# Six added matrix products between a kernel's last product and TensorE's jump to the program's end

## The chip, the cores and the metric

The kernel runs on one core of a Trainium2 chip (trn2). The metric is the device time of one execution in microseconds; lower is better. A core has five engines that run their own instruction streams side by side: TensorE (matrix products, PE in the rows, with its weight loads as PEld), VectorE (DVE), ScalarE (ACT), GpSimd (POOL) and SyncE (SP, which here only starts transfers). Each engine has a sequencer that hands the instructions of its stream to the engine; rows of the sequencer carry a q behind the engine's name (PEldq, POOLq). The engines wait for each other through counting semaphores, and move data between memory and chip through 16 DMA engines that several queues share.

## What is computed

The reference is a block-sparse attention over 4 batches of 768 positions with 8 heads of 64, followed by a mixture of 8 experts in which each token goes to one expert:

```python
def reference(**kwargs):
    attn_out = _attn_ref(**attn_kwargs)          # window of 16 and 24 block summaries, softmax, times v
    x = attn_out.transpose(0, 2, 1, 3).reshape(B, S, H * D)
    return _moe_ref(x=x, **moe_kwargs)
...
# _moe_ref, per token: e is the best expert, or the one before if a local gate says so
h = np.maximum(x[b, s] @ w1[e], 0.0)             # 512 -> 1024
out[b, s] = p[e] * (h @ w2[e])                   # 1024 -> 512
```

## The kernel before

The first half of the program is the attention; the second half sorts the 3072 tokens by expert into blocks of 128 rows and runs the expert layers block by block. A block's rows are gathered (`gather`), turned (`tx`), multiplied with the expert's first weights (`pair_1`, `quad`, `single_parts.mm1`), passed through a relu (`relu`, or an activation in `mm1`), multiplied with the second weights (`second`, `single_parts.mm2`), scaled by the gate and scattered to their rows of the output (`store`, `scatter`). Every weight and every input of a product is held as a high and a low part, so that one product of the mathematics is three on TensorE: `mm`, lines 1147 (high times high), 1148 (high times low) and 1149 (low times high), each 128 x 128 by 128 x 512.

The order of the work is written out by hand: each engine executes its instructions as the code issues them, and a layer under the code adds the semaphore waits. How many blocks there are depends on the data. `run` holds two versions of the second half: the usual one (line 1616, `tc.If(...) as usual`), which is the one executed here, and a general one behind `usual.Else()` in line 1625. The general one follows the usual one in each engine's stream, so every engine leaves the usual version with a jump over the general one (the jump carries line 1616) to the code after both, which is the program's end.

The usual version ends in `pair_and_single`, line 1346: a pair of blocks, and with it a single last block. The last thing it does on TensorE is `mm2(range(2, 8))`, eighteen products into the bank `ya` (the `ba` of the rows). GpSimd meanwhile makes the last low parts of the second weights in four steps (line 1109), and line 1148 waits for them. The last block is not stored inside the version: `store(..., late=True)` only copies its indices and gates (lines 1155 and 1156), and behind the two versions stand, for both,

```python
nc.gpsimd.drain()                     # line 1628
self.last_rows()                      # line 1629: ya * gate -> yl on VectorE (line 1167),
                                      # then the scatter of yl on GpSimd (line 1171)
```

What stands behind the two versions has to wait for either of them. The layer under the code therefore brings each engine's count to one value at the end of both versions, and line 1167 waits until TensorE's count (PE_49) has that value, that is, until the last product of the version that ran. Then comes the program's end (line 1715), where SyncE waits for the transfers and all engines meet. Products of other lines that the text names: `few_3` (line 1224) multiplies a few rows with weights, inside a condition (line 1560).

Of the kernel before, what the change touches and what calls it, by code (L numbers as in the profile page):

```python
# [19 lines left out]
P = 128  # L20
# [68 lines left out]
class Kernel:  # L89
# [1268 lines left out]
    def run(self):  # L1358
        nc, tc = self.nc, self.tc
# [44 lines left out]
        def freed():  # L1404
            st["free"] += 1
            ask_rows()
# [32 lines left out]
        def reg(i, engines, hi):  # L1439
            return nc.values_load(self.words[0:1, i:i + 1], engines=engines, min_val=0, max_val=hi)  # L1440

        def refill(w, nxt):

            with tc.If(nxt > 0):  # L1444
                e = nc.s_assert_within(nxt - 1, 0, E - 1, skip_runtime_bounds_check_because="the branch is taken for 1 to E alone")
                for h in range(2):
                    self.fetch(st["stage"][w][:, 2048 * h:2048 * h + 2048], w, 2048 * h, 2048 * h + 2048, e)

        def split(w, chunks):
            for q in chunks:  # L1450
                eng = nc.vector if SPLIT_BY[w][q] == "V" else nc.gpsimd
                self.split(w, q * CH, q * CH + CH, st["stage"][w][:, q * CH:q * CH + CH], eng)

        def calls(n, mids={}, sure=False):

            r = {}

            def start(s):
                while "words" not in st:
                    self.small(1, True)  # L1460
                if s not in r:
                    r[s] = reg(s, (ENG.SP, ENG.Activation, ENG.DVE, ENG.Pool), 1), reg(COLS + s, (ENG.SP,), E)
                return r[s]

            def weights(w, s, chunks):
                if not EARLY <= s < SLOTS:
                    return
                new, nxt = start(s)
                with tc.If(new > 0):  # L1469
                    split(w, chunks)  # L1470
                    if chunks[-1] == NCH - 1:
                        refill(w, nxt)

            def turn(u):
                while st["next"] <= u:
                    self.small(1, True)
                if u % 2 and u >= 2 * PAIRS and not sure:
                    with tc.If(reg(u, (ENG.PE, ENG.Activation, ENG.DVE), 1) > 0):
                        self.tx(u)
                else:  # L1480
                    self.tx(u)
                freed()
                if sure and u + 1 in EMPTY:
                    assert st["next"] > u + 1
                    freed()

            mids = {j: lambda u=u: turn(u) for j, u in mids.items() if u < SLOTS}
            return mids, lambda *chunks: weights(0, n, chunks), lambda *chunks: weights(1, n, chunks)
# [17 lines left out]
        with ExitStack() as ctx:  # L1506
# [67 lines left out]
            def run(gen, n0=0):  # L1574
                n = n0
                for n, _ in enumerate(gen, n0):
                    steps.get(n, int)()
                return n + 1
# [37 lines left out]
            with tc.If(known[2 * COLS + 1] < LATE + 5 - EARLY) as usual:  # L1616
                n = 0
                for (i, k), (j, m) in zip(USUAL, USUAL[1:]):
                    if k > 2:
                        n = run(self.quad(i, k, *calls(j, dict(zip(PMU, range(j, j + m + (j == LATE)))), True)), n)  # L1620
                    elif k == 2:
                        nc.gpsimd.drain()  # L1622
                        run(self.pair_and_single(i, *calls(j)), n)
            st.update(kept)
            with usual.Else():
                slots(EARLY, LATE)
# [93 lines left out]
```

## Time and profile before

| what | us |
|---|---|
| median of 3 timed runs | 414.23 (413.96 to 414.83) |
| profiled execution, its own time | 417.37 |
| its span, first to last instruction | 415.6 |
| TensorE busy | 401.2 (97% of the span) |
| VectorE, ScalarE, GpSimd busy | 232.8, 186.9, 199.1 |
| mean granted TensorE clock | 0.997 of full speed |

The three timed runs lie 0.87 us apart. The span of the profiled execution is 1.77 us shorter than its own time, and that time is 3.14 us above the median of the timed runs. Times inside the profile count from the span's start. A busy TensorE row of 0.39 us is one product with its fill and drain; the next one starts before it has ended, so the pace is read from the starts.

### The profile page before, as it was taken

The numbers are of one execution on the slowest core, as the hardware profiler recorded it, in microseconds if no ns is written. First come the engines' busy times: TensorE is split into PE (matmuls) and PEld (weight loads), VectorE is DVE, ScalarE is ACT, GpSimd is POOL, SyncE is SP. The second block draws the span as 40 slices with busy tenths as digits, with TensorE's granted clock in tenths as the row PEclk, the third lists the DMA queues.
The fourth block names the chain that finished last, engine by engine and source line by source line (L and its number), as shares of the span: only waits on it lengthen the run. The fifth ranks groups of instructions, "written<-read, shape, count | busy, mean of one in ns | idle before, by whom it ended". The sixth has DMA issues, their size and how long they took to land. (4 is left out here: it accounts for less than half of the span.)

```text
span 415.6 us, 10447 instructions
## 1 busy us (share of the span) xinstructions
PE 401.2 (97%) x3802; PEld 332.5 (80%) x3802; DVE 232.8 (56%) x516; ACT 186.9 (45%) x461; POOL 199.1 (48%) x334
## 2 busy tenths in 40 slices
PE   7999999999999999999999999999999999999993
PEld 6678777778798888888877877888998888889882
DVE  4778978989687777685232222263537433312631
ACT  4978877788874322156221002251535422101550
POOL 7599877877769300258503310063716460010552
PEclk9999999999999999999999999999999999999998
DMA  8999999999490200857777464128353670010011
GB/s 298 412 410 407 410 401 409 386 377 334 109 353 32 84 26 0 337 224 252 267 275 250 135 222 147 83 53 294 93 186 108 233 223 35 26 53 25 2 49 34
DMA packets 21936, 83.70 MB, mean 201 GB/s; under 512 B 2638, under 2 KB 3152, under 8 KB 18800
## 3 DMA queue, kind: packets, MB, share of 16 engines
q1 hardware_dynamic: 17600, 68.49, 44.2%
q0 software_dynamic: 4128, 14.22, 9.9%
q8 instruction: 32, 0.52, 0.5%
q10 hardware_dynamic: 144, 0.20, 0.2%
q14 instruction: 32, 0.26, 0.2%
HBM read 69.43 MB, written 13.60 MB: 200 GB/s over the span
## 5 line engine op out<-in xcount | busy, mean ns | idle before, releaser
L1253 ACT ACTIVATE hT<-bs 128x256 fp32r<-128x256 f32 (+1 forms) x88 | 34.6, 394 | 116.2 <-PE bs L1292 64.2
L1255 DVE SCALAR_TENSOR_TENSOR hT<-bs,hT 128x256 fp32r<-128x256 f32 (+1 forms) x88 | 38.3, 435 | 72.1 <-ACT hT L1253 72.0
L1147 PE MATMUL ba<-h,hT 128*128 128x512 f32 x192 | 77.9, 406 | 0.0
L1149 PE MATMUL ba<-h,hT 128*128 128x512 f32 x192 | 75.1, 391 | 0.0
L1148 PE MATMUL ba<-l,hT 128*128 128x512 f32 x192 | 74.9, 390 | 0.0
L1171 POOL DMA_INDIRECT out_dram<-yo,sidx x23 | 25.7, 1116 | 77.3 <-DVE yo L1163 36.7
L1290 PE MATMUL bs<-xT,h 128*128 128x512 f32 (+1 forms) x160 | 61.1, 382 | 0.0
L1291 PE MATMUL bs<-xT,h 128*128 128x512 f32 (+1 forms) x160 | 60.6, 379 | 0.0
L1292 PE MATMUL bs<-xT,l 128*128 128x512 f32 (+1 forms) x160 | 60.6, 379 | 0.0
L1118 POOL DMA_INDIRECT xg<-x_dram,gidx x26 | 30.0, 1154 | 62.6 <-PE ba L1149 27.5
L384 ACT ACTIVATE pr<-bs,nm 128x120 f32<-128x120 f32 x192 | 52.1, 382 | 4.8 <-DVE nm L376 4.5
L1109 POOL TENSOR_TENSOR l<-stg,h 128x256 fp32r<-128x256 f32 x48 | 37.6, 814 | 14.9 <-ACT h L1101 14.8
L1149 PEld LDWEIGHTS ba<-h,hT 128*128 128x128 f32 x192 | 36.0, 188 | 7.9
L1147 PEld LDWEIGHTS ba<-h,hT 128*128 128x128 f32 x192 | 36.1, 188 | 7.2 <-issue 0.8
L307 POOL COPY vw<-gs 24x432 f32<-24x432 f32 (+2 forms) x83 | 34.2, 431 | 15.5 <-issue 10.9
L1148 PEld LDWEIGHTS ba<-l,hT 128*128 128x128 f32 x192 | 36.2, 188 | 6.4
L1101 ACT CAST h<-stg 128x1024 fp32r<-128x1024 f32 x32 | 32.5, 1048 | 12.8 <-PE ba L1149 9.9
L1104 DVE TENSOR_TENSOR l<-stg,h 128x1024 fp32r<-128x1024 f32 x20 | 30.3, 1525 | 10.9 <-ACT h L1101 10.6
L1290 PEld LDWEIGHTS bs<-xT,h 128*128 128x128 f32 x160 | 30.0, 188 | 5.4 <-PE bs L1205 0.4
L1291 PEld LDWEIGHTS bs<-xT,h 128*128 128x128 f32 x160 | 30.0, 188 | 5.1 <-DVE xT L1124 0.2
L1292 PEld LDWEIGHTS bs<-xT,l 128*128 128x128 f32 x160 | 30.0, 188 | 5.0
L405 PE MATMUL ba<-vw,pt 121*64 121x76 f32 x768 | 32.5, 233 | 1.2 <-DMA vt<-in_vT 0.7
(271 smaller groups left out, 676.9 us busy)
## 6 DMA issues: line engine op xcount, KB each, us to landing
stg<-in_w SPq DMA_DIRECT2D x16, 1024.0 KB, 5.7
vw<-in_vW SPq DMA_DIRECT2D x16, 768.0 KB, 10.5
raw<-in_w SPq DMA_DIRECT2D x8, 1024.0 KB, 8.2
x_dram<-xs SPq DMA_DIRECT2D x8, 876.0 KB, 9.6
kp<-in_kT SPq DMA_DIRECT2D x16, 384.0 KB, 7.8
q<-in_qT SPq DMA_DIRECT2D x16, 384.0 KB
vt<-in_vT SPq DMA_DIRECT2D x16, 384.0 KB, 9.2
wst<-in_w SPq DMA_DIRECT2D x8, 512.0 KB, 9.2
```

The source lines that it names most:

```text
L307: nc.gpsimd.tensor_copy(out=bass.AP(dst.tensor, dst.offset, [dst.ap[0], (step, planes), (4, NW), (1, m)]), in_=bass.AP(src.tensor, src.off ...
L384: nc.scalar.activation(out=pr[:, h, u, :], in_=sp[:, h, u, :], func=AF.Exp, bias=nm[:, h, u:u + 1], scale=1.0)
L405: nc.tensor.matmul(out=ap[64 * c:64 * c + 64, u, h], lhsT=pt[0:W + 1, h, u, 64 * c:64 * c + 64], rhs=vw[n % NVW][0:W + 1, PL * h:PL * h + ...
L1109: eng.tensor_tensor(out=lo[:, p], in0=src[:, p], in1=hi[:, p].bitcast(F32), op=ALU.subtract)
L1147: nc.tensor.matmul(out=ps, lhsT=ah, rhs=wh, start=first, stop=False)
L1148: nc.tensor.matmul(out=ps, lhsT=ah, rhs=wl, start=False, stop=False)
L1149: nc.tensor.matmul(out=ps, lhsT=al, rhs=wh, start=False, stop=last)
L1253: self.nc.scalar.activation(out=h, in_=ps, func=AF.Relu)
L1255: self.nc.vector.scalar_tensor_tensor(out=l, in0=ps, scalar=0.0, in1=h.bitcast(F32), op0=ALU.max, op1=ALU.subtract)
L1290: nc.tensor.matmul(out=ps, lhsT=wh, rhs=xh[k], start=(k == 0), stop=False)
L1291: nc.tensor.matmul(out=ps, lhsT=wh, rhs=xl[k], start=False, stop=False)
L1292: nc.tensor.matmul(out=ps, lhsT=wl, rhs=xh[k], start=False, stop=(k == KT - 1))
```

## The change

Inside the usual version, behind the loop over the blocks, TensorE gets six products more. They read a part of `hT[1]` and of the first weights, both in place for long, and write the same bank of the pool "t" six times; nothing reads that bank afterwards. Their form is that of line 1147 (128 x 128 by 128 x 512, high parts). Nothing else is changed. The lines behind it move down by three, so that the program's end is line 1718 instead of 1715.

```diff
@@ -1621,6 +1621,9 @@
                     elif k == 2:
                         nc.gpsimd.drain()
                         run(self.pair_and_single(i, *calls(j)), n)
+                idle = self.bank("t")
+                for _ in range(6):
+                    nc.tensor.matmul(out=idle, lhsT=self.hT[1][:, 0, 0, 0:P], rhs=self.hi[0][:, 0:512], start=True, stop=True)
             st.update(kept)
             with usual.Else():
                 slots(EARLY, LATE)
```

TensorE's stream at the end of the usual version, in one piece of the difference (`ba` is the bank `ya`, `bt` the bank that nobody reads, `h` and `l` the parts of the weights; the row of line 1273 already belongs to the general version, which is not executed):

```order
 L1148 MATMUL ba_3587<-l_2523,hT_2828 128x512 [waits Pool_49]
 L1149 MATMUL ba_3587<-h_2521,hT_2828 128x512
+L1626 MATMUL bt<-h_2520,hT_2828 128x512 x6
 L1616 UNCONDITIONAL_BRANCH [waits PE_sequencer_49]
 L1273 MATMUL bs<-xT,h_2520 128x256 [waits Activation_49]
```

The six products stand between the last product of the last block and the jump, and wait for nothing. In the built program, the step of TensorE's count that the last product of line 1149 carried stands on the sixth added product instead.

VectorE's stream at its end is the same in both (before shown):

```order
L1155 COPY il<-sidx 128x1 [waits DMASW3_49]
L1156 COPY pl<-psort 128x1 [waits DVE_49]
L1591 UNCONDITIONAL_BRANCH
L1606 UNCONDITIONAL_BRANCH [waits DVE_49,DVE_sequencer_49] x11
L1167 TENSOR_SCALAR yl<-ba_3587,pl 128x512 [waits DMASW3_49,DMASW1_49,DMASW7_49,DVE_49,PE_49]
L1715 UNCONDITIONAL_BRANCH
```

Line 1167 waits for TensorE's count at the end of the version, as it did; the six products are now part of that count.

## Rows read from the trace of the kernel before

**Rows 1.** Page, parts 1 and 3: busy us of the engines; one queue's packets, MB, share.
```profile
PE 401.2 (97%) x3802; PEld 332.5 (80%) x3802; DVE 232.8 (56%) x516; ACT 186.9 (45%) x461; POOL 199.1 (48%) x334
...
q8 instruction: 32, 0.52, 0.5%
```

**Rows 2.** Waits of SyncE's queue from 395 us: engine, line, for whom, us, times, longest.
```profile
SPq L1715 <- DMA out_dram<-yl,il: 47.0, 1, 47.0
SPq L1715 <- PEq L1715: 0.7, 2, 0.5
```

**Rows 3.** Timeline, 401.9 to 416 us: start, us, engine, line, operation, count, [idle before <-releaser].
```profile
402.25 0.39 PE L1147 MATMUL ba<-h,hT 128*128 128x512 f32 x1
...
404.05 2.84 POOL L1109 TENSOR_TENSOR l<-stg,h 128x256 fp32r<-128x256 f32 x4
...
405.20 0.40 PE L1149 MATMUL ba<-h,hT 128*128 128x512 f32 x1
...
407.02 0.39 PE L1148 MATMUL ba<-l,hT 128*128 128x512 f32 x1
...
407.93 0.39 PE L1149 MATMUL ba<-h,hT 128*128 128x512 f32 x1
408.35 0.75 DVE L1167 TENSOR_SCALAR yl<-ba,pl 128x512 f32<-128x512 f32 x1 [2.67 <-PE ba L1149]
409.38 1.00 POOL L1171 DMA_INDIRECT out_dram<-yl,il  x1 [2.50 <-DVE yl L1167]
```

**Rows 4.** DMA view, 410.9 to 411.8 us, 40 slices: GB/s by packets' starts; packets by queue.
```profile
GB/s 0 0 910 364 364 182 546 364 0 364 728 364 546 364 364 182 182 910 364 0 546 364 364 182 182 1456 364 546 182 364 182 182 1 0 0 0 1 0 0 0
DMA packets 78, 0.27 MB, mean 300 GB/s; under 512 B 15, under 2 KB 15, under 8 KB 77
q0 software_dynamic: 77, 0.25, 75.5%
q8 instruction: 1, 0.02, 9.4%
```

**Rows 5.** DMA view, 411.4 to 411.6 us, 40 slices of 5 ns.
```profile
GB/s 819 0 0 819 0 0 0 819 0 0 0 0 1638 819 4915 0 0 819 0 819 0 0 0 2458 0 0 0 0 0 0 819 819 0 819 0 0 819 0 0 0
q8 instruction: 1, 0.02, 42.1%
```

**Rows 6.** DMA view, 411.8 to 412.75 us.
```profile
DMA packets 0, 0.00 MB, mean 0 GB/s; under 512 B 0, under 2 KB 0, under 8 KB 0
```

**Rows 7.** DMA view, 412.75 to 413.6 us, 40 slices of 21 ns.
```profile
GB/s 0 0 193 0 0 0 0 0 0 0 0 0 0 0 0 0 0 0 0 0 0 0 193 0 0 0 0 0 0 0 0 0 0 0 0 0 0 0 0 0
DMA packets 3, 0.01 MB, mean 10 GB/s; under 512 B 1, under 2 KB 1, under 8 KB 3
q0 software_dynamic: 3, 0.01, 5.4%
```

**Rows 8.** Line 1616 from 402 us: engine, operation, count: ns min/median/max, first and last start.
```profile
L1616 PEldq EVENT_SEMAPHORE  x1: 51/51/51, 406.9 to 406.9; - x1
L1616 PEldq COMPARE_BRANCH  x1: 3382/3382/3382, 407.1 to 407.1; - x1
```

**Rows 9.** DMA view, 407.9 to 408.2 us, 40 slices of 7.5 ns.
```profile
GB/s 0 0 0 0 0 0 0 0 0 0 0 0 0 0 0 0 0 2185 0 0 0 0 0 0 0 0 0 0 0 0 0 0 0 0 0 0 0 0 0 0
q8 instruction: 1, 0.02, 21.9%
```

**Rows 10.** Line 1224, 266 to 272 us: its products, and the waits of TensorE's sequencer.
```profile
L1224 PE MATMUL bs<-raw,fhT x64: 272/273/297, 270.2 to 271.9; 128*32 128x128 f32 x64
L1224 PEldq EVENT_SEMAPHORE  x3: 51/51/51, 266.2 to 270.5; - x3
```

**Rows 11.** Line 1560, 266 to 272 us: the jumps around those products.
```profile
L1560 PEldq COMPARE_BRANCH  x2: 65/120/176, 266.1 to 271.4; - x2
```

**Rows 12.** Line 1147, 398.45 to 403 us: a wait of TensorE's sequencer.
```profile
L1147 PE MATMUL bs<-h,xT x4: 389/391/397, 399.5 to 401.6; 128*128 128x512 f32 x4
...
L1147 PEldq EVENT_SEMAPHORE  x1: 51/51/51, 398.5 to 398.5; - x1
```

**Rows 13.** DMA issues, whole span: count, median us from issue to landing.
```profile
out_dram<-yo,sidx POOLq DMA_INDIRECT x23, 3.0
...
out_dram<-yl,il POOLq DMA_INDIRECT x1, 4.6
```

## The prediction

> **What bounds the kernel now.** I read the page first, then the end of the trace backwards. TensorE is busy for 401.2 of 415.6 us [rows 1], but the change touches nothing before its last product, so only the tail counts. The waits of SyncE's queue say what ends the program: at its end it waits for one transfer, the scatter of yl (its 47.0 us are the whole wait), and only 0.7 us in two pieces for TensorE's sequencer [rows 2]. The timeline gives the way to that transfer: the last product starts at 407.93 and takes 0.39, so it ends at 408.32; line 1167 starts at 408.35, released by it; the scatter is issued at 409.38 [rows 3]. Whatever delays the last counted product, or the landing of this scatter, delays the end by as much.
>
> The landing holds a surprise. The scatter of yl lands 4.6 us after its issue, the 23 scatters of yo before it after 3.0 in the median [rows 13]. The DMA view shows why. The packets of the scatter start at about 410.95 (the third slice of 22.5 ns behind 410.9) and run on all 16 engines until about 411.77 [rows 4]. Then for almost a microsecond no packet starts [rows 6], and three stragglers follow in slices that begin at 412.79 (third) and 413.24 (twenty-third), the last of them, of under 512 bytes, later still, in a slice whose rate is too small to print, before 413.6 [rows 7]; I take 413.5. So one engine was held, for about 1.7 us beyond the others. In the middle of the scatter stands one packet of another kind: 0.02 MB on queue q8, instructions, in the fifteenth slice of 5 ns behind 411.4, at 411.47. It took 42.1% of 16 engines' 0.2 us, which is 1.35 us on one engine [rows 5], up to 412.82, where the stragglers begin.
>
> **Whose packet is it?** Queue q8 has 32 packets in 0.52 MB, 16 KB each [rows 1]. TensorE's jump to the end starts at 407.1 and takes 3382 ns, to 410.5 [rows 8]. One q8 packet starts 0.9 us behind its start (eighteenth slice behind 407.9: 408.03) and takes 21.9% of 16 x 0.3 us, 1.05 us [rows 9]; the second starts 1.0 us behind the jump's end. Both hang on this jump, and I read them as the page of code jumped to and the page after it. The Trainium skill, "Runtime: NRT & Kernel Launch", section "Instruction fetch mechanics", says that code comes in blocks of 16 KiB (256 instructions), that the sequencer itself fetches the next page while it executes the current one, and that a taken jump out of the window forces a fetch. By its figure the 3802 products and 3802 loads of rows 1 would be 30 pages, an estimate; the trace has 32 packets and agrees.
>
> So the change moves two things: the store, which waits for the six products, and the fetch, which follows the jump. What matters is by how much each moves.
>
> **The store moves by 1.37 us.** The six products have line 1147's form and wait for nothing. From 405.20 to 407.93 there are twelve steps of this form, 2.73 us, 0.2275 each [rows 3]; six are 1.37 us. A product that did not overlap with its neighbour would cost 0.39, six 2.3; nothing in the last twelve steps suggests it. Line 1167 waits for TensorE's count, and the step that satisfies it stands on the sixth added product, so line 1167, the scatter and its first packets move by 1.37: packets from 412.31, fifteen engines done at 413.13. Line 1167 hides nothing of it: VectorE sits idle 2.67 us before it.
>
> **The fetch moves by about 0.16 us.** A sequencer runs ahead of its engine, so the question is how fast six more products pass through it. Its wait in front of the jump is at 406.9 [rows 8], when five products have still to start (407.02 to 407.93 [rows 3]). What it had stood at just before is GpSimd's last low part: four steps from 404.05 take 2.84, to 406.89 [rows 3], and the second-last product waits for it. From 406.89 to its wait at 406.9 (at most 406.95, as the row is rounded) it handed over the last two products, four instructions with their loads, in at most 0.06 us. A second place gives the same rate: few_3's second half is 32 products and 32 loads between the wait at 270.5 and the jump at 271.4 [rows 10, 11]; less 51 ns that is 0.85 us by 64, 13 ns each. Twelve instructions more are 0.16 us. Is there room for them ahead of the engine? At 398.5 the sequencer already stands at a wait of line 1147 that belongs to the product at 402.25 [rows 3, 12]: the four line 1147 products of bs lie between them, each with two others, so it was over a dozen products ahead. Eleven products with their loads, the queue behind the change, are less than that. So the jump starts at about 407.25, ends at 410.63, and the second page is fetched from about 411.63, alone on its engine for 1.05 (the price of rows 9), to 412.68.
>
> **The sum.** The scatter's packets come at 412.31, 0.37 us before that engine is free. Its share of packets needs as long as on the others, 0.82 (410.95 to 411.77), so it lands at 413.50. Before, it landed at 413.5. In other words: +1.37 for the products, -1.74 for the hole that closes (413.5 less 411.77), +0.37 for the new contact, together 0.0. Bounds of the contact: none (fetch done before 412.31), and the whole sum is -0.37; or a fetch of 1.35 as in rows 5, to 412.98, +0.67, and packets as slow as the stragglers (0.45 between two, rows 7), another 0.5, and the sum is +0.8. Those slow packets I put at a third of that, +0.1 in all. The profiled execution would be at 417.4 again, and the timed median at 414.23 + 0.1 = 414.3. What else the change adds is hidden: the jump's end at 410.63 has until the meeting of the engines, past 413.5, and if that cover were gone TensorE's 0.7 us of rows 2 would grow by the 0.16. The products' bank was last read by VectorE before 406, their operands are long in place.
>
> **Rivals.** (a) **The jump moves with the products**, because the sequencer can't get ahead of them after all. Then the fetch moves by 1.37 like the store, the contact is the old one, and the end is 1.37 later: 415.6, slower. It decides from the point where the fetch starts behind the first packets on its engine, 412.31, that is, from a delay of the jump of 0.84 us instead of 0.16. For it: the lead is only five products in rows 8; against it: that lead is explained by GpSimd, and rows 10 to 12 show the longer ones. (b) **The timed executions have no contact before**: the fetch hit the last two packets or so of its engine (it started 0.3 us before the others were done), and the timed runs are 3.14 us shorter than the profiled one. If there it comes 0.3 us later, the kernel before loses nothing, and after the change the fetch, 1.2 us earlier against the store, lands in front of it: +1.37 and a contact of at least 0.5, 416.1, up to the full hole of 1.74, 417.3. (c) **No contact is left after the change**: -0.37, 413.9, inside 0.2%. (d) **The products do not hold the store**, that is, the change does not do what I read: then the store stays, the fetch moves to 411.63, behind most of its packets, and up to 1.74 goes: 412.5, faster. Against it stands the built program's count.
>
> The Trainium skill, "TensorE: Matmul & The Clock Gate", section "Architectural detail", gives TensorE's queue 64 places, so that twelve more instructions would not hold the jump; by this the sum stays 0.0, and by a queue as short as the lead of rows 8 it would be rival (a). The dozen products of rows 12 agree with the page.
>
> **How the numbers follow.** A measurement of this kernel tells about 0.2% (0.83 us) from no change: 413.4 to 415.06. My forecast, a new contact of 0 to 1.2 us with the sum between -0.37 and +0.8, takes rival (c) in and has 0.66 (0.54 and 0.12); (a) 0.16, (b) 0.13, (d) and anything else that is faster 0.05. Slower is (a) and (b), 0.29; same 0.66. The range runs from (c), less 0.1 for the spread of runs, to (a), with as much on top: 413.8 to 415.7; (b) and (d), 0.18 together, stay outside.
>
> **What would show it.** After the change: six products of line 1626 at 0.23 us steps, the first where line 1149's last one ends its turn (408.16); line 1167 at 409.7; TensorE's jump still near 407.2 and not at 408.5; q8's second packet near 411.6, ahead of the scatter's packets from 412.3; no hole of a microsecond in the scatter, and a landing of some 3.2 us instead of 4.6. A jump at 408.4 or a second hole makes (a) right. A profile as I say with a timed median above 415.2 makes (b) right. A line 1167 at 408.4 makes (d) right.

## The result, and the profile after

The change makes the kernel slower: 416.57 us median against 414.28, ratio 1.0053 with an interval of 1.0036 to 1.007. The forecast was 414.3, no change. What happened is rival (b), to which I had given 0.13: the trace of the changed kernel looks as forecast in the main, and the timed runs are slower nevertheless, inside its price (416.1 to 417.3).

The mechanism first. The timeline of the kernel after (start, us, engine, line, operation, count) answers to [rows 3]:

```profile
406.88 0.39 PE L1149 MATMUL ba<-h,hT 128*128 128x512 f32 x1
...
407.11 1.52 PE L1626 MATMUL bt<-h,hT 128*128 128x512 f32 x6
408.67 0.75 DVE L1167 TENSOR_SCALAR yl<-ba,pl 128x512 f32<-128x512 f32 x1 [4.04 <-PE bt L1626]
409.70 1.00 POOL L1171 DMA_INDIRECT out_dram<-yl,il  x1 [3.83 <-DVE yl L1167]
```

The last real product starts at 406.88, line 1167 at 408.67, 1.79 us later; in [rows 3] it was 0.42. The store is held by 1.37 us, as worked out, and the releaser is now the product of line 1626. All other times of this trace lie about 1 us earlier than before at the same place of the program; that much the executions differ by ahead of the tail, so only distances inside the tail are compared.

Line 1616 of the kernel after (ns, first and last start), beside [rows 8]:

```profile
L1616 PEldq EVENT_SEMAPHORE  x1: 51/51/51, 405.9 to 405.9; - x1
L1616 PEldq COMPARE_BRANCH  x1: 3442/3442/3442, 406.1 to 406.1; - x1
```

The jump starts at 406.1, ahead of the last real product by 0.8 us, as before (407.1 against 407.93). The six products did not take it with them. Its second page of code, in the DMA view of 410.2 to 410.4 us (40 slices of 5 ns), starts in the twelfth slice, at 410.26:

```profile
GB/s 0 0 0 0 0 0 0 0 0 0 0 3277 0 0 0 0 0 0 0 0 0 0 0 0 0 0 0 0 0 0 0 0 0 0 0 0 0 0 0 0
...
q8 instruction: 1, 0.02, 38.7%
```

It takes 1.24 us (38.7% of 16 engines' 0.2 us), to 411.50. The scatter's first packet comes at 411.27, in the eighth slice of 10 ns behind 411.2, 0.23 us before that engine is free. Where its packets end, the DMA view of 411.9 to 412.3 us has

```profile
DMA packets 19, 0.02 MB, mean 41 GB/s; under 512 B 15, under 2 KB 15, under 8 KB 19
```

and that of 412.3 to 412.7 us

```profile
DMA packets 2, 0.00 MB, mean 10 GB/s; under 512 B 1, under 2 KB 1, under 8 KB 2
```

The sixteen packets of 4 bytes (the ones under 512 bytes) close the scatter, one behind each engine's share of the data. Fifteen of these closing packets start before 412.3, at 412.09 the latest, and the last at 412.5, 0.4 us late. The scatter lands 3.3 us after its issue (4.6 in [rows 13]). So the profiled execution after is even shorter than the profiled one before (416.36 against 417.37). It is the wrong comparison: 417.37 is not what the kernel before usually takes.

### The profile page after: what moved, and what is told of

It reads as the page before. It is cut to its first block, busy times and chain, and to the rows that moved or that the text cites. A ratio compares the mean times of both kernels' runs of the same rounds, so it can differ in the third digit from the quotient of the medians.

```text
span 414.6 us, 10459 instructions
## 1 busy us (share of the span) xinstructions
PE 401.3 (97%) x3808; PEld 333.3 (80%) x3808; DVE 232.9 (56%) x516; ACT 187.4 (45%) x461; POOL 198.8 (48%) x334
```

## Experiments

The hole is the stretch of about a microsecond in which one engine's rest of the scatter waits behind the fetched page. Theory A is rival (b): the timed executions of the kernel before have no hole, or only some of them have one, so the products' 1.37 us and the new contact are lost on top of an undisturbed tail. The rivals: B, the hole is in every execution and each product costs some 0.38 us; C, no contact matters to the timed runs at all. Runs of one batch share their runs of the kernel before; between batches (other chips) its median went from 414.28 to 415.91, so differences are taken inside a batch.

### Four more traces of the kernel before

No edit.

> The kernel before once more, to see in a second trace whether its last scatter has the hole. Theory A (the timed executions of before have no contact: TensorE's second page of code starts behind the last packets of the scatter, so the change has no hole to close, and its own new contact comes on top of the 1.37 us): this trace shows no hole, the scatter lands about 3.0 us after its issue instead of 4.6, and the profiled execution's own time is nearer to 414.3 than to 417.4. Theory B (the hole of 1.74 us is in every execution, and the six products cost about 0.38 us each for another reason): the hole is there again. Both: 414.3 us, ratio 1.000.

> The kernel before, one more trace. Theory A: whether the scatter of yl has a hole goes with where TensorE's second page of code starts. Starting up to 0.8 us behind the scatter's first packet it makes a hole, and the landing is 4 us or more; starting later than that it makes none, and the landing is 2.7 us. Executions of the second kind are the usual ones (about three in four). Theory C: the hole is in every execution of before.

> As the look before it: a third trace of the kernel before; no hole in about three of four (theory A), a hole every time (theory C).

> As the two looks before it: a fourth trace of the kernel before.

With the trace of before there are five. The times of starts are read from DMA views of short stretches. The last column is the tail: the own time less the start of the last real product (some 1.8 us of it lie outside the span, alike in all).

| trace | own time, us | jump took, ns | second page starts behind the scatter's first packet, us | landing, us | tail, us |
|---|---|---|---|---|---|
| before | 417.37 | 3382 | 0.52 | 4.6 | 9.44 |
| e1 | 416.69 | 3420 | 1.11 | 4.7 | 9.53 |
| third look | 417.19 | 3402 | 0.82 | 4.4 | 9.24 |
| second look | 415.75 | 3560 | 1.32 | 2.9 | 7.77 |
| fourth look | 415.71 | 3889 | 0.79 | 2.7 | 7.58 |

The first of the four went against theory A as I had put it: I expected no hole in e1, and there is one. Only then did A become "in some executions, about one in four", which the other three traces test.

DMA view of the third look, 411.7 to 411.9 us (slices of 5 ns):

```profile
GB/s 0 0 2 1 0 0 1 0 0 0 1 0 1 0 1 0 0 0 3277 1 0 0 0 0 0 0 0 0 0 0 0 0 0 0 0 0 0 0 0 0
DMA packets 9, 0.02 MB, mean 82 GB/s; under 512 B 8, under 2 KB 8, under 8 KB 8
```

The same view from 411.85 to 413.2 us:

```profile
DMA packets 2, 0.00 MB, mean 3 GB/s; under 512 B 1, under 2 KB 1, under 8 KB 2
```

DMA view of the second look, 410.9 to 412.2 us:

```profile
DMA packets 80, 0.26 MB, mean 202 GB/s; under 512 B 16, under 2 KB 16, under 8 KB 80
```

And from 412.2 to 412.4 us:

```profile
GB/s 0 0 0 0 0 0 0 0 0 0 0 0 0 0 0 0 0 0 0 0 0 0 3277 0 0 0 0 0 0 0 0 0 0 0 0 0 0 0 0 0
q8 instruction: 1, 0.02, 29.0%
```

In the third look the page comes while small closing packets are going out; one engine still has a data packet and its closing packet to do, and they wait for it. In the second look all 80 packets of the scatter are through before the page starts at 412.31. Three traces have the hole and two have none; on the chip of the last three, the third look took 1.4 us more than the two others. A hole in every execution, theory B's (and that of C in the expectations of these looks), is out, and a contact that comes and goes by this much is what C has no place for. My border was wrong in detail: in e1 the page came 1.11 us behind, not 0.8, and still held one packet of 4 bytes for 1.2 us (the landing came 2.0 us later than the undisturbed 2.7; where the other 0.8 went is not shown), while in the fourth look it came at 0.79 and met an engine that had finished. So it takes both, when the page starts and how far its engine has come. The jump took 3382 to 3420 ns in the traces with the hole and 3560 and 3889 in those without, but the second page starts 0.7 to 1.6 us behind the jump's end, and five traces do not say which of these decides. The timed runs do not show how frequent the hole is. In the batch of e1, 22 of the 29 lie between 414.03 and 414.89 and seven between 415.13 and 416.1, but no clear gap parts them, and the last real product itself starts anywhere from 407.16 to 408.13 in the five traces. My three in four is not shown.

The tails do say which kind the median belongs to. With a hole, 414.28 less 9.24 to 9.53 would put the last real product at 405.0 at the latest; in the fourteen traces of all the versions here its earliest start is 406.75. Without a hole, 7.58 to 7.77, it is 406.5 to 406.7. This is an estimate, since the batch of the result has no trace of an undisturbed execution; the other reading misses every trace by 1.7 us.

### Six again, and three

```diff
-                for _ in range(6):
+                for _ in range(3):
```

> The six products once more. Theory A (products 1.37 us on the path, and the second page of code now runs into the head of the scatter in most executions, which it did to the kernel before in a few only): 1.37 and 0.3 to 0.9 above the usual 414.5 of before, 416.2 to 416.8 us, and a landing some 0.4 us longer than undisturbed in the trace. Theory C (no contact matters in the timed executions; the six products alone make the whole difference at some 0.35 us each): the same total, so this run only sharpens the number that the next three share out.

> Three products in place of six. The store moves by 0.68 us, the jump by 0.08, so the second page of code comes 0.6 us earlier against the scatter than before and falls into its middle. Theory A: 0.68 and a hole of 0.8 to 1.4, 416.0 to 416.6 us, hardly less than with six. Theory C: half of the difference of six, 415.6 us.

Six: 417.15 against 415.8 in its batch, ratio 1.0038 (1.0021 to 1.0055). Three: 417.2, ratio 1.0036 (1.0019 to 1.0054). Half the products cost as much. Both lie above the ranges that I had set, on a chip where the kernel before is 1.2 us slower than in the batch of e1; what came out is "hardly less than with six". The 1.35 us of the six products here would be the products alone; that before has the hole more often in this batch, whose runs reach 417.75, is likely and not shown. The DMA view of the three products, 411.4 to 411.6 us (slices of 5 ns):

```profile
GB/s 0 0 0 0 0 0 0 0 0 0 0 0 0 0 0 0 3277 0 0 0 0 0 0 0 0 0 0 0 0 0 0 0 0 0 0 0 0 0 0 0
...
q8 instruction: 1, 0.02, 38.2%
```

The same view, 411.7 to 413.8 us (slices of 52.5 ns):

```profile
GB/s 78 468 312 234 624 234 312 546 312 234 546 312 312 156 0 0 0 0 0 78 0 0 0 0 0 0 78 0 0 0 0 0 78 0 0 78 0 0 0 0
```

And the landing of the scatter among its DMA issues:

```profile
out_dram<-yl,il POOLq DMA_INDIRECT x1, 4.0
```

The page starts at 411.48, 0.27 us ahead of the scatter, and is in the way for 1.22 us; four data packets come one by one between 412.70 (twentieth slice) and 413.6. The store is held 0.68 us less than by six products, and the landing, 4.0 against 3.3, takes as much more. C, which had half the difference for half the products (0.68 us, where the interval of three starts at 0.8), falls. The tails of the three products and of the six are the same 9.52 us.

### The store alone, without work on TensorE

```diff
             nc.gpsimd.drain()
+            for _ in range(2):
+                nc.vector.tensor_scalar(out=self.yl, in0=self.ya, scalar1=self.pl, scalar2=None, op0=ALU.mult)
             self.last_rows()
```

> No products; VectorE does line 1167's operation twice more before it, so the store comes 1.4 to 1.5 us later (two times 0.75, less the overlap) and the jump stays. For the fetch against the store this is the same shift as that of the six products, without any work on TensorE. Theory A: 1.45 and the new contact of 0.4 to 0.9, 416.2 to 416.7 us, as the six products. Theory B: 1.45 less the hole that closes, 414.1 us.

416.48 us against 414.62, ratio 1.0039 (1.0027 to 1.0051). Timeline:

```profile
407.22 1.54 DVE L1630 TENSOR_SCALAR yl<-ba,pl 128x512 f32<-128x512 f32 x2 [2.68 <-PE ba L1149]
408.80 0.75 DVE L1167 TENSOR_SCALAR yl<-ba,pl 128x512 f32<-128x512 f32 x1
```

Landing among the DMA issues:

```profile
out_dram<-yl,il POOLq DMA_INDIRECT x1, 3.2
```

Line 1167 comes 1.58 us late and the landing takes 0.5 us more than an undisturbed one of 2.7; the time rises by 1.86, inside the 416.2 to 416.7 of theory A. The six products do to the end what any delay of the store by that much does.

The DMA view of 410.3 to 410.5 us (slices of 5 ns) shows that this contact is not only a wait for the page:

```profile
GB/s 0 0 0 0 0 0 0 0 0 0 3277 0 0 0 0 0 0 0 0 0 0 0 0 0 0 0 0 0 0 0 0 0 0 0 0 0 0 0 0 0
...
q8 instruction: 1, 0.02, 32.1%
```

The page starts at 410.35 and takes 1.03 us, to 411.38, and the scatter's first packet comes at 411.40. Nothing waits for the page, and still one engine's first data packet takes 0.62 us instead of the usual 0.17, and the last closing packet is 0.4 us late. That this is the page's engine is likely; the trace does not name the engine.

### The store further away: twelve

```diff
-                for _ in range(6):
+                for _ in range(12):
```

> Twelve products in place of six. The store moves by 2.73 us, the jump by about 0.3, so the second page of code (some 411.8 to 412.9 on the profile's clock) is through well before the scatter's first packet (413.7). Theory A: only the 2.73 are left, 417.0 us, at most 417.4, hence only 0.4 to 0.8 above the six products. Theory B (0.38 us a product): 418.9 us.

417.24 us against 414.62, 2.62 more (A: 2.7). The timeline:

```profile
407.59 2.88 PE L1626 MATMUL bt<-h,hT 128*128 128x512 f32 x12
410.51 0.75 DVE L1167 TENSOR_SCALAR yl<-ba,pl 128x512 f32<-128x512 f32 x1 [5.40 <-PE bt L1626]
```

The landing:

```profile
out_dram<-yl,il POOLq DMA_INDIRECT x1, 2.7
```

The landing is undisturbed: the page of code is through at 412.1, a microsecond before the scatter's first packet. Twelve products are twelve times 0.227 us and nothing else, and the six runs lie within 0.7 us. B (418.9) falls.

The jump, and the last real product, with twelve products:

```profile
L1616 PEldq COMPARE_BRANCH  x1: 3382/3382/3382, 406.6 to 406.6; - x1
407.36 0.39 PE L1149 MATMUL ba<-h,hT 128*128 128x512 f32 x1
```

The jump still begins 0.75 us ahead of the last real product; in the five traces of before it is 0.78 to 0.84. So 24 instructions more move it by about 0.06 us, some 3 ns each.

### The jump alone

`reg` reads a register from memory in TensorE's sequencer, which holds the jump and leaves TensorE's count alone.

```diff
                         run(self.pair_and_single(i, *calls(j)), n)
+                for _ in range(2):
+                    reg(2 * COLS, (ENG.PE,), SLOTS)
```

With six reads, with two (twice), and with three behind the six products:

> No products; in their place TensorE's sequencer reads a register from memory six times in front of its jump, so that the jump alone comes later (six times about 0.3 us, some 2 us) and the store stays where it was. The second page of code then starts near 413.5 on the profile's clock, behind the scatter (411.8). Theory A: nothing to gain, 414.3 us (within 0.3). Theory B: the hole closes, 1.7 us less, 412.6 us.

> No products, two register reads in front of the jump: the jump comes 1.4 us later and ends some 1 us ahead of the end's meeting, so that neither the page of code nor the jump's end is in the way. Theory A: the kernel before without its slow quarter: the median a little lower, 414.3 to 414.6 us, and no run above 415.5 (before had seven of 29 above 415.2). Theory C: the times of before, slow quarter and all.

> The two register reads in front of the jump again, to see whether the gain of 0.2% holds. Theory A: 0.1 to 0.2% below before, less spread, no hole and a landing of 2.7 us in the trace. Theory C: no difference.

> The six products, and behind them three register reads by TensorE's sequencer in front of the jump (0.68 us each in the run with six reads), so that the second page of code starts 2.0 us later and behind the scatter. The jump would end near 412.7 on the clock of the profile before, over a microsecond ahead of the end's meeting. Theory A: the contact is gone and 1.37 is left, 415.9 us. Theory C: nothing changes against the six products, 416.6 us.

Six reads: 416.21 against 414.62, which neither theory had. Line 1616 there:

```profile
L1616 PEldq COMPARE_BRANCH  x1: 3457/3457/3457, 410.0 to 410.0; - x1
```

The waits of SyncE's queue, beside [rows 2]:

```profile
SPq L1717 <- DMA out_dram<-yl,il: 45.1, 1, 45.1
SPq L1717 <- PEq L1717: 2.6, 2, 2.0
```

A read took 0.7 us and not the 0.3 that I had set, because of the register work and the check behind it, so the jump began at 410.0, ended at 413.4, and the end of the program waited for TensorE (2.6 us in place of the 0.7 of [rows 2]). The scatter itself was undisturbed, 2.7 us to its landing. The cover that the prediction named for the jump's end is real, and it is used up a little over 2 us behind the usual place: the jump began some 4 us later against the last product than before (3.2 us behind its start, not 0.8 ahead), and some 1.5 to 1.9 of that were waited for.

Two reads stay inside it: 415.36 against 415.8, ratio 0.9981 (0.9966 to 0.9996), with no run above 415.78, where 19 of the 35 runs of before are. On a third chip it was 415.54 against 415.91, ratio 0.9992 (0.9977 to 1.0006), which does not exclude zero. In the first of the two traces the jump starts at 407.8, half a microsecond behind the last product instead of ahead of it, and ends at 411.1, and the landing is undisturbed:

```profile
out_dram<-yl,il POOLq DMA_INDIRECT x1, 2.7
```

My range (414.3 to 414.6) and my limit of 415.5 for it were missed, since that chip is a microsecond slower altogether. In the second trace the landing takes 3.0 us, where I had 2.7, although the page starts 0.9 us behind the last packet: landings that no page disturbs spread from 2.7 to 3.0. The version with two reads is the one here that is ahead of both kernels, by 0.1 to 0.2% of the kernel before, and only one of the two measurements is clear of zero.

The six products with three reads behind them: 416.54, ratio 1.002 (1.0007 to 1.0032), 0.6 us below the six products alone on the same chip, where C had no difference; the 415.9 that I had set for A was missed by as much on this slower chip. Its jump starts at 408.1, and its landing is undisturbed as well:

```profile
out_dram<-yl,il POOLq DMA_INDIRECT x1, 2.7
```

Against the two reads of the same batch, whose tail is undisturbed too, the products alone cost 1.18 us (1.37 by the timeline), and with the contact, 417.15, they cost 1.79. That is 1.37 and some 0.4, as the packets of the trace of after have it; its landing, 3.3 against 2.7 to 3.0, has 0.3 to 0.6.

## Why the prediction was wrong

- **The products hold the store by 1.37 us.** Right: 1.79 less 0.42 in the timelines; twelve cost 2.62.
- **The jump does not move with them, and the page comes ahead of the scatter.** Right: the jump is still 0.8 us ahead of the last real product. The 0.16 us for its delay was too much: against the last real product it moved by no more than 0.05 us. The 13 ns an instruction behind it was TensorE's own pace (the 64 products of [rows 10] are 27 ns apart, two instructions each) and not the sequencer's, which the twelve products put at some 3 ns. I had put the page 0.68 us ahead of the scatter's first packet (411.63 against 412.31); it is 1.01 ahead in the trace of after (410.26 against 411.27) and 0.66 in the second one.
- **The new contact, 0.37 us.** Right in size: the last packet is 0.4 us late in both traces. But only 0.2 to 0.3 of it is the wait for the page, and the rest is the data packet behind it, which takes 0.52 us where others take 0.17; I had put slow packets at 0.1. The landing takes 3.3, which is 0.3 to 0.6 more than an undisturbed one.
- **"-1.74 for the hole that closes".** This step failed. The hole was taken from the one profiled execution and booked against the median. The kernel before has it in some executions only (three traces of five); its median, 414.28, belongs to the kind without it, by the tails. From the last real product to the end the kernel after takes 9.48 us, and 9.52 in its second trace. Against the 9.24 to 9.53 of executions with the hole that is the 0.0 of my sum, and against the 7.58 to 7.77 of those without it is 1.7 to 1.9 more. Without this term my own sum is 1.37 and 0.37, 416.0 for a median of 414.28; measured 416.57, with an interval that reaches from 1.5 to 2.9 us. The warning stood in the table ahead of it: the profiled execution took 3.14 us longer than the median of the timed runs. The hole, 1.74, is the larger part of that; the rest is a last product that comes later.
- **The range.** It ended at rival (a) and left (b) out as the less likely one. (b) is what was found, at a price inside its bounds, although (b) had the fetch "0.3 us later" as a shift between profiled and timed runs. What the traces show is a spread among executions.
- **The length of the queue and the fetch.** The Trainium skill, "TensorE: Matmul & The Clock Gate", section "Architectural detail", with its 64 places in TensorE's queue, led to the same result as the rows did: the jump began at 406.1, a microsecond before the first of the added products (407.11). On code fetches, the Trainium skill, "Runtime: NRT & Kernel Launch", section "Instruction fetch mechanics", speaks of a stall of the engine that jumps; here that stall (3.44 us in the trace of after) is hidden, and what costs is the fetched page's place on a DMA engine.

What stays open is why the fetch comes earlier in one execution of the kernel before than in the next; no run set that.

## What to carry to other kernels

A stall seen in one profiled execution is a gain to be had only if the timed runs have it too: compare the profiled time with theirs first, and look at a second and third trace before it is booked. Work that nobody reads is not off the path if a wait behind it counts instructions, as that of line 1167 behind the conditional versions does here. And the last transfer of a program should not start while an engine's jump is still fetching code: move one of the two. Here that was worth 0.1 to 0.2%, and only one of two measurements of it is clear of zero.

## What the runs showed of the hardware

A page of code of 16 KB takes 0.93 to 1.4 us on one DMA engine, and a packet queued there waits for all of it: in e1 a packet of 4 bytes came 1.2 us behind the fifteen others of its kind, and the whole program waited for it. The first data packet behind such a page took 0.43 to 0.53 us in five traces, where others take 0.17. TensorE's jump over the general version took 3.28 to 3.89 us in the fourteen traces, nearly all of it hidden except with six reads, and drew two such pages, 0.9 to 1.5 us behind its start and 0.7 to 1.6 us behind its end. Handing over an instruction took TensorE's sequencer some 3 ns at the end of the usual version, a register read with its check 0.7 us.
